# Retention and a gated feed-forward layer on one core: from full score matrices to 128-position chunks with a carried state

## The chip, the core and the metric

The kernel runs on one core of a Trainium2 chip. Five engines of that core work side by side, each through its own queue of instructions in order, and meet through semaphores: TensorE (PE) multiplies matrices, with the loads of its weights shown as a row of their own (PEld); VectorE (DVE), ScalarE (ACT) and GpSimd (POOL) work element by element; SyncE (SP) here only starts transfers. The transfers themselves run on 16 DMA engines. The metric is device time in microseconds for one execution.

## The reference

Inputs are q, k and v in fp32, shaped 8 batches x 8 heads x 576 positions x 64, and two weight matrices, 512 x 2048 and 2048 x 512. The output is 4608 x 512 in fp32.

```
scores = (q @ k.T) / 8                       # per batch and head
Dmat[i, j] = gamma_h ** (i - j)  if i >= j else 0,   gamma_h = 1 - 2 ** (-5 - h)
x = (scores * Dmat) @ v                      # then heads side by side: 4608 x 512
h = x @ w_in                                 # 4608 x 2048
g = h * clip(h + 3, 0, 6) / 6
out = g @ w_out                              # 4608 x 512
```

There is no softmax: a head's output is a causal sum in which older positions fade by a fixed factor per step.

## The kernel before

**Attention.** The kernel goes through batches, and in each batch through four pairs of heads (the loop over `c`). For a pair it loads q, k and v of both heads from DRAM with a cast to fp16 on the way (`cast_load`, line 97; the transfers are issued by POOL, one per head and tensor, 128 x 5 x 64 elements). TensorE transposes q and k in blocks of 128 positions (line 174), VectorE and ScalarE copy the transposes out of PSUM (lines 178, 180). Then the whole lower half of the 576 x 576 score matrix of each head is formed, transposed, in bands of 128 key positions (line 200); VectorE multiplies each band with a table of decay factors for every distance and head, `dmask`, and writes fp16 (line 210). The bands are multiplied with v (line 230), and ScalarE copies the result into `xt16`, which holds x transposed for all 4608 tokens (line 236). The two heads of a pair use rows 0 to 63 and 64 to 127 of the array in the score products, and columns 0 to 63 and 64 to 127 in the products with v.

**The table.** At the start POOL builds the distances (`rsel`) and ScalarE turns them into `dmask` with eight exponentials of 128 x 1600 elements (line 80).

**The feed-forward part.** Tokens are taken in nine blocks of 512. `moe_unit` with kind 0 is one up unit: four matmuls of 128 x 512 into one PSUM bank (line 122), a relu on ScalarE (line 126) and the gating on VectorE (line 128), which writes a slice of `gt16`. With kind 1 it is one down unit: 16 matmuls for 128 tokens (line 136), a copy by ScalarE (line 140) and a store of 256 KB (line 141, issued by SP). The weights are loaded by POOL in three pieces during the first batch, cast to fp16 on the way (lines 243, 246).

**Order.** `chunkq` is the list of units whose tokens are ready, and `pop_units` issues a few of them at fixed places between the parts of a head pair, so that TensorE has large matmuls beside attention. A block becomes ready only when the batch that holds its last token is finished. From this program order a scheduler derives the order on each engine. All PSUM tiles come from one pool of eight banks. What remains in `chunkq` after the last batch follows without attention beside it.

Of the kernel before, what the change touches and what calls it, by code (L numbers as in the profile page):

```python
# [14 lines left out]
ALU = mybir.AluOpType  # L15


@with_exitstack
def kernel(
# [13 lines left out]
    P = 128  # L33

    NCH = (S + P - 1) // P
    msz = [min(P, S - P * i) for i in range(NCH)]
    m1sub = []
    for tcix in range(NCH):
        lo = P * tcix
        subs = []  # L40
        while lo < S:
            hi = min(lo + 512, S)
            subs.append((lo, hi))
            lo = hi
        m1sub.append(subs)
    atoff = []
    o = 0
    for tcix in range(NCH):
        atoff.append(o)
        o += S - P * tcix  # L50
    ATW = o
    m2sc = [(0, 288), (288, 576)]

    gamma = [1.0 - 2.0 ** (-5.0 - h) for h in range(H)]
    NFULL = S // P
    REM = S - NFULL * P

    const = ctx.enter_context(tc.tile_pool(name="const", bufs=1))
    work = ctx.enter_context(tc.tile_pool(name="work", bufs=3))
    big = ctx.enter_context(tc.tile_pool(name="big", bufs=1))  # L60
# [3 lines left out]
    cb = const.tile([P, 2], FP32)  # L64
    nc.gpsimd.memset(cb[:, 0:1], 0.5)
    nc.gpsimd.memset(cb[:, 1:2], float(np.log(0.125)))

    rsel = const.tile([P, ATW], FP32)
    for tcix in range(NCH):
        W = S - P * tcix  # L70
        nc.gpsimd.iota(rsel[:, atoff[tcix]:atoff[tcix] + W],
                       pattern=[[1, W]], base=0, channel_multiplier=-1,
                       allow_small_or_imprecise_dtypes=True)
        nc.gpsimd.affine_select(
            out=rsel[:, atoff[tcix]:atoff[tcix] + W],
            in_=rsel[:, atoff[tcix]:atoff[tcix] + W], compare_op=ALU.is_ge,
            fill=1.0e8, base=0, pattern=[[1, W]], channel_multiplier=-1)
    dmask = const.tile([P, H, ATW], FP16)
    for h in range(H):
        nc.scalar.activation(dmask[:, h, :], rsel, ACTF.Exp,  # L80
                             bias=cb[:, 1:2], scale=float(np.log(gamma[h])))

    win16 = big.tile([P, DM // P, DFF], FP16)
    wout16 = big.tile([P, DFF // P, DM], FP16)

    NCC = DM // P
    xt16 = big.tile([P, NCC, NTOK], FP16)

    psum = ctx.enter_context(tc.tile_pool(name="psum", bufs=8, space=bass.MemoryType.PSUM))

    def cast_load(src4, b, h, dst, coloff, width):
        last = (b == B - 1 and h == H - 1)
        if not last:
            fl = src4[b, h].rearrange("s d -> (s d)")
            ap = bass.AP(tensor=fl.tensor, offset=fl.offset,
                         ap=[[D, P], [P * D, NCH], [1, D]])
            nc.gpsimd.dma_start(dst[:, :, coloff:coloff + D], ap)
        else:
            nc.gpsimd.dma_start(
                dst[:, 0:NFULL, coloff:coloff + D],  # L100
                src4[b, h, 0:NFULL * P, :].rearrange("(j p) d -> p j d", p=P))
            nc.gpsimd.dma_start(dst[0:REM, NFULL, coloff:coloff + D],
                                src4[b, h, NFULL * P:S, :])
            nc.gpsimd.memset(dst[REM:P, NFULL, coloff:coloff + D], 0.0)

    NFC = DFF // P
    MBLK = 512
    NMB = NTOK // MBLK
    chunkq = []
    moe_state = {}  # L110

    def moe_unit(kb, kind, ix):
# [30 lines left out]
    def pop_units(n):  # L143
        for _ in range(n):
            if chunkq:
                moe_unit(*chunkq.pop(0))
# [142 lines left out]
```

## Time and profile before

| | |
|---|---|
| three runs | 450.07, 449.37, 449.47 us; median 449.47 |
| the profiled execution | span 448.7 us from the first to the last instruction; its own time is not listed beside it |
| matmuls | 2368, of which 576 up and 576 down with 512 columns each |
| moved | read 39.80 MB, written 9.44 MB |
| loads of q, k, v and weights | issued by POOL, 129,488 packets |
| stores | issued by SP, 5184 packets, 36 transfers of 256 KB, 2.0 us to landing |

PE, PEld, DVE, ACT, POOL and SP are the engines' names in the profile; L122 is line 122 of the kernel. A row of the slices gives the busy tenths of an engine in 40 equal parts of the span; PEclk is the clock that TensorE was granted, in tenths of full speed. The chain is followed back from the last instruction, at each step to what released it. In a list of groups or a timeline, "out<-in" names the tiles, and "64*128 64x512" is a matmul on 64 rows and 128 columns of the array with 512 moving columns. A share of the DMA engines above 100% means that transfers overlap on them.

### The profile page before, as it was taken

What the parts mean: (1) busy time and instruction counts of PE and PEld (TensorE: products, weight loads), DVE (VectorE), ACT (ScalarE), POOL (GpSimd) and SP (SyncE); (2) the same over time, 40 slices, a digit from 0 to 9 for tenths busy, and PEclk for the clock granted to TensorE, in tenths of its full rate; (3) what the DMA queues carried; (4) which work ended last, traced back from release to release, by engine and by line L of the source; (5) the groups of instructions that cost most, each with busy time, mean ns of one, the idle gap of its engine ahead of it and who ended that gap; (6) DMA issues with size and microseconds to landing.
All of it is one profiled execution on the core that took longest, in us unless ns stands there. A gap on an engine that the chain in (4) does not pass through costs nothing.

```text
span 448.7 us, 6207 instructions
## 1 busy us (share of the span) xinstructions
PE 394.0 (88%) x2368; PEld 181.7 (40%) x2368; DVE 230.5 (51%) x432; ACT 201.6 (45%) x349; POOL 177.6 (40%) x222
## 2 busy tenths in 40 slices
PE   0387999989998999899998999899989999899996
PEld 0133444434443444444443444344443444344442
DVE  0254675347716672467635771667245763480540
ACT  5623564156522663356415652266325641571641
POOL 9966799763534444155326353445200000000000
PEclk9999999999998999999999999999998999999999
DMA  5999999985777766487568568776210001001101
GB/s 36 123 189 192 120 96 96 154 75 37 46 92 88 46 45 61 86 55 50 37 101 74 39 44 93 87 50 42 39 70 1 0 1 70 26 0 48 47 23 70
DMA packets 134700, 29.73 MB, mean 66 GB/s; under 512 B 126480, under 2 KB 130064, under 8 KB 134672
## 3 DMA queue, kind: packets, MB, share of 16 engines
q0 software_dynamic: 129488, 19.91, 60.8%
q1 hardware_dynamic: 5184, 9.44, 5.7%
q8 instruction: 18, 0.29, 0.3%
q14 instruction: 10, 0.08, 0.1%
HBM read 39.80 MB, written 9.44 MB: 110 GB/s over the span
## 4 chain that ended last, share of the span: by engine, by line
PE 69%; DVE 18%; ACT 9%; issue 2%; POOL 1%; DVEq 0%; POOLq 0%
PE pout L136 28%; PE ph L122 22%; DVE at16a L210 8%; DVE at16b L210 6%; PE pst L174 5%; ACT dmask L80 3%; ACT xt_104 L236 2%; ACT u L126 2%; ACT sb L180 2%; DVE gt_6_3580 L128 1%; DVE gt_5_3055 L128 1%; DVE gt_0_430 L128 1%; DVE gt_4_2530 L128 1%; DVE gt_3_2005 L128 1%; DVE gt_2_1480 L128 1%
## 5 line engine op out<-in xcount | busy, mean ns | idle before, releaser
L122 PE MATMUL ph<-xt_104,win_102 128*128 128x512 f16 x576 | 143.2, 383 | 5.7 <-DVE gt_1_955 L128 0.8
L126 ACT ACTIVATE u<-ph,cb 128x512 f32<-128x512 f32 x144 | 97.2, 687 | 53.2 <-PE ph L122 51.0
L122 PEld LDWEIGHTS <-win_102 128*128 128x128 f16 x576 | 52.6, 97 | 71.0 <-issue 19.5
L140 ACT COPY osb<-pout 128x512 f32<-128x512 f32 x36 | 21.1, 585 | 111.5 <-PE pout L136 111.5
L178 DVE COPY sb<-pst 128x576 f16<-128x576 f16 x32 | 14.5, 455 | 43.3 <-PE pst L174 43.3
L200 PEld LDWEIGHTS <-sb 64*128 64x128 f16 (+1 forms) x384 | 14.9, 100 | 42.5 <-ACT sb L180 18.2
L180 ACT COPY sb<-pst 128x576 f16<-128x576 f16 x32 | 20.4, 637 | 3.6 <-PE pst L174 1.6
L128 DVE SCALAR_TENSOR_TENSOR gt_8_4320<-u,ph 128x512 f16<-128x512 f32 x16 | 11.0, 688 | 16.6 <-ACT u L126 16.6
L128 DVE SCALAR_TENSOR_TENSOR gt_6_3580<-u,ph 128x512 f16<-128x512 f32 x16 | 10.7, 681 | 9.0 <-ACT u L126 8.9
L128 DVE SCALAR_TENSOR_TENSOR gt_2_1480<-u,ph 128x512 f16<-128x512 f32 x16 | 10.5, 679 | 9.2 <-ACT u L126 9.2
L128 DVE SCALAR_TENSOR_TENSOR gt_5_3055<-u,ph 128x512 f16<-128x512 f32 x16 | 10.7, 681 | 8.0 <-ACT u L126 7.8
L128 DVE SCALAR_TENSOR_TENSOR gt_4_2530<-u,ph 128x512 f16<-128x512 f32 x16 | 10.7, 681 | 8.0 <-ACT u L126 7.8
L128 DVE SCALAR_TENSOR_TENSOR gt_0_430<-u,ph 128x512 f16<-128x512 f32 x16 | 10.5, 680 | 8.3 <-ACT u L126 8.3
L128 DVE SCALAR_TENSOR_TENSOR gt_1_955<-u,ph 128x512 f16<-128x512 f32 x16 | 10.5, 680 | 8.1 <-ACT u L126 8.1
L128 DVE SCALAR_TENSOR_TENSOR gt_3_2005<-u,ph 128x512 f16<-128x512 f32 x16 | 10.5, 680 | 8.1 <-ACT u L126 8.1
L136 PE MATMUL pout<-wout_103,gt_2_1480 128*128 128x512 f16 x64 | 14.3, 379 | 0.2 <-DVE at16a L210 0.2
L136 PE MATMUL pout<-wout_103,gt_4_2530 128*128 128x512 f16 x64 | 14.3, 379 | 0.2 <-DVE at16a L210 0.2
L136 PE MATMUL pout<-wout_103,gt_0_430 128*128 128x512 f16 x64 | 14.3, 379 | 0.2 <-DVE at16a L210 0.2
L136 PE MATMUL pout<-wout_103,gt_1_955 128*128 128x512 f16 x64 | 14.3, 379 | 0.2 <-DVE at16a L210 0.2
L136 PE MATMUL pout<-wout_103,gt_5_3055 128*128 128x512 f16 x64 | 14.3, 379 | 0.2 <-DVE at16a L210 0.2
L136 PE MATMUL pout<-wout_103,gt_6_3580 128*128 128x512 f16 x64 | 14.3, 379 | 0.2 <-DVE at16a L210 0.2
L136 PE MATMUL pout<-wout_103,gt_3_2005 128*128 128x512 f16 x64 | 14.3, 379 | 0.2 <-DVE at16a L210 0.2
(1059 smaller groups left out, 775.9 us busy)
## 6 DMA issues: line engine op xcount, KB each, us to landing
out_dram<-osb SPq DMA_DIRECT2D x36, 256.0 KB, 2.0
win_102<-in_moe_w_in_dram POOLq DMA_DIRECT2D x2, 640.0 KB, 8.8
wout_103<-in_moe_w_out_dram POOLq DMA_DIRECT2D x2, 640.0 KB, 10.0
win_102<-in_moe_w_in_dram POOLq DMA_DIRECT2D x1, 768.0 KB, 9.9
wout_103<-in_moe_w_out_dram POOLq DMA_DIRECT2D x1, 768.0 KB, 10.5
qn_108<-in_q_dram POOLq DMA_DIRECT2D x2, 80.0 KB, 3.0
kn_109<-in_k_dram POOLq DMA_DIRECT2D x2, 80.0 KB, 3.0
vn_110<-in_v_dram POOLq DMA_DIRECT2D x2, 80.0 KB, 3.1
```

Source lines behind the costliest of these rows:

```text
L80: nc.scalar.activation(dmask[:, h, :], rsel, ACTF.Exp, bias=cb[:, 1:2], scale=float(np.log(gamma[h])))
L122: nc.tensor.matmul(ph, win16[:, dmc, P * fc:P * fc + P], xt16[:, dmc, tok0:tok0 + MBLK], start=(dmc == 0), stop=(dmc == NCC - 1))
L126: nc.scalar.activation(u, ph, ACTF.Relu, bias=cb[:, 0:1], scale=1.0 / 6.0)
L128: nc.vector.scalar_tensor_tensor(out=gt16[:, fc, :], in0=u, scalar=1.0, in1=ph, op0=ALU.min, op1=ALU.mult)
L136: nc.tensor.matmul(pout, gt16[:, fc, P * mc:P * mc + P], wout16[:, fc, :], start=(fc == 0), stop=(fc == NFC - 1))
L140: nc.scalar.copy(osb, pout)
L174: nc.tensor.transpose(pst[:, P * j:P * j + sj], nat[0:sj, j, :], ident16[0:sj, 0:sj])
L178: nc.vector.tensor_copy(sb, pst)
L180: nc.scalar.copy(sb, pst)
L200: nc.tensor.matmul(pms[h2][0:mt, co:co + ns], kt2[base:base + D, P * tcix:P * tcix + mt], qt2[base:base + D, a:bb], start=True, stop=True)
L210: nc.vector.tensor_tensor(out=at16s[h2][0:mtg, alo:alo + wid], in0=pms[h2][0:mtg, 0:wid], in1=dmask[0:mtg, 2 * c + h2, alo:alo + wid], op= ...
L236: nc.scalar.copy(xt16[h2 * D:h2 * D + D, c, b * S + s0:b * S + s1], pos[h2][h2 * D:h2 * D + D, 0:s1 - s0])
```

## The change

The attention part is written anew, and the order of the whole kernel with it.

The 4608 tokens are cut into 36 chunks of 128 positions. `load(c)` fetches k, q and v of a chunk for all eight heads in fp32, with SP issuing (256-byte rows; a chunk that lies across a batch border takes two transfers per tensor). `casts(c)` makes fp16: k on ScalarE, q on POOL (on VectorE for the first four chunks), v on POOL; q is multiplied with gamma^p/8 and v with gamma^-p, where p is the position in the chunk less 64, so that the decay inside the chunk comes out of the product itself and the mask holds only ones and zeros. `transposes(c)` makes q and k transposed: by TensorE for chunks 0 to 3, by a transposing DMA issued from SP for the others.

Inside a chunk, `scores(c)` and `inner(c)` do the causal product; what earlier chunks of the batch contribute comes from a 64 x 64 state per head. `state(c)` forms k^T v of the chunk, VectorE adds the previous state, POOL multiplies with gamma^128 (`gpow`) and copies the result into `sbd`, a block-diagonal fp16 tile for the two heads of a pair; `inner` of the next chunk multiplies it with q and adds it in PSUM. A chunk that lies across a batch border uses a second mask and, for its state, a second v whose first half is zero (`vz`).

`visit(c)` is the unit of order: it issues the loads up to chunk c+5, casts and transposes up to chunk c+1, the scores of c, the product with v of chunk c-1 and the state of c. The order on TensorE is that of the program throughout, on POOL only up to the first up product. Five visits come first, with the weight loads between them in 24 pieces; then the 16 up units of block 0 with a visit after every fourth; then, for each block, an up unit of the next block and four matmuls of the down product of this one in turn, with a visit after every fourth unit until chunk 36 is past. A down product holds two PSUM banks at a time and stores 512 KB per pair of 128-token tiles.

```diff
--- before
+++ after
...
+def segments(c):
+    n0 = P * c
+    b, s0 = divmod(n0, S)
+    if s0 + P <= S:
+        return [(b, s0, P, 0)]
+    m = S - s0
+    return [(b, s0, m, 0), (b + 1, 0, P - m, m)]
+straddle = [len(segments(c)) > 1 for c in range(NCH)]
+has_state = [segments(c)[0][1] > 0 for c in range(NCH)]
+gives_state = [c + 1 < NCH and has_state[c + 1] for c in range(NCH)]
+keeps_state = [has_state[c] and not straddle[c] for c in range(NCH)]
...
+io = ctx.enter_context(tc.tile_pool(name="io", bufs=4))
+work = ctx.enter_context(tc.tile_pool(name="work", bufs=3))
+gp = ctx.enter_context(tc.tile_pool(name="gp", bufs=6))
+psum = ctx.enter_context(tc.tile_pool(name="psum", bufs=8, space=bass.MemoryType.PSUM))
...
+arg = const.tile([P, 2 * H], FP32)
+dec = const.tile([P, 2 * H], FP32)
+nc.scalar.activation(dec, arg, ACTF.Exp)
...
+gpow = const.tile([P, NP], FP32)
...
+mask = const.tile([P, 2, P], FP16)
...
+sbd = []
...
+win16 = const.tile([P, NP, DFF], FP16)
+wout16 = const.tile([P, NFC, DM], FP16)
...
+def load(c):
+    tiles = []
+    for nm, src in (("k", k), ("q", q), ("v", v)):
+        t = io.tile([P, H, D], FP32, tag=f"f{nm}", name=f"f{nm}{c}")
+        for (b, s0, n, p0) in segments(c):
+            nc.sync.dma_start(t[p0:p0 + n], src[b, :, s0:s0 + n, :].rearrange("h s d -> s h d"))
+        tiles.append(t)
+    st[c] = dict(f=tiles)
+def casts(c):
+    fk, fq, fv = st[c]["f"]
+    k16 = work.tile([P, H, D], FP16, tag="k16", name=f"k16_{c}")
+    q16 = work.tile([P, H, D], FP16, tag="q16", name=f"q16_{c}")
+    v16 = work.tile([P, H, D], FP16, tag="v16", bufs=4, name=f"v16_{c}")
+    nc.scalar.copy(k16, fk)
+    qe = nc.vector if c < PE_T else nc.gpsimd
+    qe.tensor_tensor(q16, fq, dec[:, 0:H].unsqueeze(2).to_broadcast([P, H, D]), ALU.mult)
+    nc.gpsimd.tensor_tensor(v16, fv, dec[:, H:2 * H].unsqueeze(2).to_broadcast([P, H, D]), ALU.mult)
+    st[c].update(k16=k16, q16=q16, v16=v16, vz=v16)
+    if straddle[c] and gives_state[c]:
+        vz = work.tile([P, H, D], FP16, tag="vz", bufs=1, name=f"vz_{c}")
+        nc.gpsimd.tensor_tensor(vz, fv, decz.unsqueeze(2).to_broadcast([P, H, D]), ALU.mult)
+        st[c]["vz"] = vz
+def transposes(c, on_pe):
+    for nm in ("k", "q"):
+        src = st[c][nm + "16"].rearrange("p h d -> p (h d)")
+        dst = work.tile([P, NP, P], FP16, tag=f"{nm}T", name=f"{nm}T_{c}")
+        if on_pe:
+            pt = psum.tile([P, NP, P], FP16, tag="pp", name=f"pt{nm}{c}")
+            for i in range(NP):
+                nc.tensor.transpose(pt[:, i, :], src[:, i * P:(i + 1) * P], ident16)
+            nc.vector.tensor_copy(dst, pt)
+        else:
+            nc.sync.dma_start_transpose(dst, src)
+        st[c][nm + "T"] = dst
+def scores(c):
+    kT, qT = st[c]["kT"], st[c]["qT"]
+    a16 = work.tile([P, 2, NP, P], FP16, tag="a16", name=f"a16_{c}")
+    pa = [psum.tile([P, NP, P], FP32, tag="pp", name=f"pa{h2}_{c}") for h2 in range(2)]
+    for i in range(NP):
+        for h2 in range(2):
+            r = slice(h2 * D, h2 * D + D)
+            nc.tensor.matmul(pa[h2][:, i, :], kT[r, i, :], qT[r, i, :], start=True, stop=True)
+    m = mask[:, int(straddle[c]):int(straddle[c]) + 1, :].to_broadcast([P, NP, P])
+    for h2 in range(2):
+        nc.vector.tensor_tensor(a16[:, h2], pa[h2], m, ALU.mult)
+    st[c]["a16"] = a16
+def state(c):
+    if not gives_state[c]:
+        return
+    k16, vz = st[c]["k16"], st[c]["vz"]
+    pu = psum.tile([P, NP, 2, D], FP32, tag="pp", name=f"pu{c}")
+    for i in range(NP):
+        nc.tensor.matmul(pu[:, i], k16[:, 2 * i:2 * i + 2, :], vz[:, 2 * i:2 * i + 2, :],
+                         start=True, stop=True)
+    z = work.tile([P, NP, D], FP32, tag="z", bufs=2, name=f"z{c}")
+    g = gpow.unsqueeze(2).to_broadcast([P, NP, D])
+    t = work.tile([P, NP, D], FP32, tag="t", bufs=2, name=f"t{c}")
+    for h2 in range(2):
+        r = slice(h2 * D, h2 * D + D)
+        if keeps_state[c]:
+            nc.vector.tensor_tensor(t[r], pu[r, :, h2, :], prev_z[0][r], ALU.add)
+        else:
+            nc.vector.tensor_copy(t[r], pu[r, :, h2, :])
+    nc.gpsimd.tensor_tensor(z, t, g, ALU.mult)
+    prev_z[0] = z
+    s = sbd[(c + 1) % 2]
+    for h2 in range(2):
+        r = slice(h2 * D, h2 * D + D)
+        nc.gpsimd.tensor_copy(s[r, :, h2, :], z[r])
+def inner(c):
+    kb = c // 4
+    if kb not in xts:
+        xts[kb] = work.tile([P, NP, BLK], FP16, tag="xT", bufs=3, name=f"xT{kb}")
+    a16, v16, qT = st[c]["a16"], st[c]["v16"], st[c]["qT"]
+    po = psum.tile([P, NP, P], FP32, tag="pp", name=f"po{c}")
+    n = P // 2 if straddle[c] else P
+    s = sbd[c % 2]
+    for i in range(NP):
+        for h2 in range(2):
+            nc.tensor.matmul(po[h2 * D:h2 * D + D, i, :], v16[:, 2 * i + h2, :], a16[:, h2, i, :],
+               start=(i == 0), stop=not has_state[c], skip_group_check=True)
+    if has_state[c]:
+        for i in range(NP):
+            nc.tensor.matmul(po[:, i, 0:n], s[:, i], qT[:, i, 0:n],
+               start=False, stop=True, skip_group_check=True)
+    o = (c % 4) * P
+    nc.scalar.copy(xts[kb][:, :, o:o + P], po)
...
+def up_unit(kb, u):
+    jj, r = divmod(u, 4)
+    half_i, jr = divmod(r, 2)
+    fc = 2 * jj + jr + JH * half_i
+    if r == 0:
+        gt[kb, jj] = [gp.tile([P, 2, BLK], FP16, tag=f"g{x}", bufs=n, name=f"g{x}{kb}_{jj}")
+                      for x, n in (("a", 8), ("b", 8))]
+    g = gt[kb, jj][half_i]
+    ph = psum.tile([P, BLK], FP32, tag="pp", name=f"ph{kb}_{fc}")
+    for dmc in range(NP):
+        nc.tensor.matmul(ph, win16[:, dmc, P * fc:P * fc + P], xts[kb][:, dmc, :],
+                         start=(dmc == 0), stop=(dmc == NP - 1))
+    uu = work.tile([P, BLK], FP32, tag="u", bufs=3, name=f"u{kb}_{fc}")
+    nc.scalar.activation(uu, ph, ACTF.Relu, bias=half, scale=1.0 / 6.0)
+    nc.vector.scalar_tensor_tensor(out=g[:, jr, :], in0=uu, scalar=1.0, in1=ph,
+                     op0=ALU.min, op1=ALU.mult)
...
+def down_plain(kb):
+    for m2 in range(2):
+        pd = [psum.tile([P, DM], FP32, tag="pp", name=f"pd{kb}_{m2}{m}") for m in range(2)]
+        o = out_tile(kb, m2)
+        for jj in range(4):
+            for m in range(2):
+                t0 = P * (2 * m2 + m)
+                for hf in range(2):
+                    for jr in range(2):
+                        nc.tensor.matmul(pd[m], gt[kb, jj][hf][:, jr, t0:t0 + P],
+                           wout16[:, 2 * jj + jr + JH * hf, :],
+                           start=(jj == 0 and hf == 0 and jr == 0),
+                           stop=(jj == 3 and hf == 1 and jr == 1))
+                        yield
+        for m in range(2):
+            nc.scalar.copy(o[:, m, :], pd[m])
+        nc.sync.dma_start(out_pair(kb, m2), o)
+def win_piece(jj):
+    sl = lambda ap: ap.rearrange("p cc (h j f) -> p cc h j f", h=2, f=2 * P)[:, :, :, jj, :]
+    for dmc in range(NP):
+        nc.gpsimd.dma_start(sl(win16)[:, dmc], sl(win_v)[:, dmc])
+def wout_piece(jj):
+    for hf in range(2):
+        fc = JH * hf + 2 * jj
+        nc.gpsimd.dma_start(wout16[:, fc:fc + 2, :], wout_v[:, fc:fc + 2, :])
+PE_T = 4
+AHEAD = 6
...
+def visit(c):
+    fetch(c + AHEAD)
+    prepare(c + 2)
+    if c < NCH:
+        scores(c)
+    if 0 <= c - 1:
+        inner(c - 1)
+    if c < NCH:
+        state(c)
+with tc.manual_schedule(engines={ENG.PE}):
+    with tc.manual_schedule(engines={ENG.Pool}):
+        fetch(2)
+        prepare(1)
+        win_piece(0)
+        fetch(4)
+        prepare(2)
+        win_piece(1)
+        visit(0)
+        win_piece(2)
+        visit(1)
+        win_piece(3)
+        for c in range(2, 5):
+            wout_piece(c - 2)
+            visit(c)
+        wout_piece(3)
+    for u in range(NFC):
+        up_unit(0, u)
+        if u in (3, 7, 11, 15):
+            visit(5 + u // 4)
+    for kb in range(NB):
+        down = down_plain(kb)
+        base = 4 * (kb + 2) + 1
+        for u in range(NFC):
+            if kb + 1 < NB:
+                up_unit(kb + 1, u)
+            for _ in range(4):
+                next(down, None)
+            if u % 4 == 2 and kb + 2 < NB:
+                visit(base + u // 4)
+        for _ in down:
+            pass
```

## The prediction

> **What bounds the kernel now.** I read the busy times first, then the slices, then the chain that ended last, then the same chain in order of time, and last the DMA queues in a stretch where loads run flat out.
>
> The page: totals, the slices and the shares of the chain.
>
> ```profile
> span 448.7 us, 6207 instructions
> PE 394.0 (88%) x2368; PEld 181.7 (40%) x2368; DVE 230.5 (51%) x432; ACT 201.6 (45%) x349; POOL 177.6 (40%) x222
> PE   0387999989998999899998999899989999899996
> ...
> PEclk9999999999998999999999999999998999999999
> ...
> PE 69%; DVE 18%; ACT 9%; issue 2%; POOL 1%; DVEq 0%; POOLq 0%
> ```
>
> TensorE is busy in 88% of the span, at full granted clock, and carries 69% of the chain; the other 31% are moments in which it waits for VectorE or ScalarE inside attention. No other engine is above 51%.
>
> The chain in order of time gives the price of each kind of work (columns: start, length in us, what).
>
> ```profile
> 46.14 0.29 PE po_404 L230
> ...
> 47.88 0.54 PE ph L122 x2
> ...
> 247.75 0.82 PE pst L174 x10
> ...
> 252.18 0.60 DVE at16b L210
> 252.78 0.60 DVE at16a L210
> 253.38 0.60 DVE at16b L210
> ...
> 431.04 13.83 PE pout L136 x64
> ```
>
> 64 matmuls of 128x512 take 13.83 us: 216 ns each. Ten transposes of 128 columns, with a weight load each, take 0.82 us: 82 ns each. The first up matmul starts at 47.88, so everything before it is head; the masking runs of VectorE are waits of TensorE.
>
> TensorE's own timeline shows how two heads share the array (start, length, what).
>
> ```profile
> 250.34 0.39 PE L200 MATMUL pm_2614<-sb 64*128 64x512 f16 x1
> 250.34 0.39 PE L200 MATMUL pm_2615<-sb 64*128 64x512 f16 x1
> 250.56 0.19 PE L200 MATMUL pm_2620<-sb 64*128 64x64 f16 x1
> 250.56 0.19 PE L200 MATMUL pm_2621<-sb 64*128 64x64 f16 x1
> ```
>
> Matmuls of the two heads, on 64 rows each, start together and cost one. The DMA answer for 60 to 76 us, when only loads run:
>
> ```profile
> DMA packets 12260, 1.56 MB, mean 97 GB/s; under 512 B 12258, under 2 KB 12258, under 8 KB 12258
> q0 software_dynamic: 12258, 1.53, 150.9%
> ```
>
> 12,258 packets in 16 us are 766 per us, and POOL, which issued them back to back, set that pace: the rings can do at least this. Over the whole page the same queue shows 129,488 packets in 60.8% of 16 engines' 448.7 us: 33.7 ns of one engine per packet, overlaps counted twice, so at worst 475 per us.
>
> **The sum of before.** Up and down products: 1152 x 0.2158 = 248.6 us. Head to the first up matmul: 47.9. After the last matmul (444.9): copy 0.58, store, 3.8 in all. The rest, 448.7 - 248.6 - 47.9 - 3.8 = 148.4 us, is attention of the 28 head pairs after the first batch, waits included: 5.3 us per pair. The median of the runs is 449.47; the span is 0.8 below it, and I add 0.8 at the end.
>
> **The change, part by part.** The 1152 large matmuls stay: 248.6 us. Per 128-position chunk, `visit` now issues 24 matmuls of 128 columns: eight scores, eight products with v (both in pairs of half the array), four for the carried state, four for the new state. If a pair costs one, 16 x 82 ns = 1.3 us; if not, 24 x 82 = 2.0. Bare streaming would be 16 x 54 = 0.9. The pairs at 250.34 are nearest, so I take 1.3. Between a 512-column run and attention TensorE lost about 0.1 us (eight matmuls from 248.50 end at 250.23 by 216 ns each; scores start at 250.34); four such changes per visit make 1.7 us (ends 0.9 and 2.4). Five visits fall into the head and 31 after it: 31 x 1.7 = 52.7 us, in place of 148.4.
>
> The masking waits of before (the lines at16a and at16b) do not come back: the scores of chunk c are used by `inner` a whole visit later. Visits lie four up-and-down units apart, 4 x 8 x 0.216 = 6.9, plus 1.7: 8.6 us. In that time VectorE has 4 gatings (0.68), 2 masks (0.68) and 2 half-height state sums (bounded by 0.68): 5.4 at most. ScalarE has 4 relus (0.69) and 3 copies (0.59): 4.5. These are covered while visits stay 8.6 apart. In the first block of up products there is no down product beside them, and visits come 3.5 + 1.7 = 5.2 us apart; there VectorE's 5.4 is as long as TensorE's run. The state chain (two VectorE operations, the POOL scaling, two POOL copies, behind two POOL casts) is also about 5. I add 3 us there (0 to 8). Two down tiles hold a PSUM bank each for eight units; the other six serve four tiles of a visit and the up tiles, each free again after 0.69 + 0.68 us, so I add nothing.
>
> POOL: 192 of the old load issues at about 0.9 us leave. It gets per chunk the casts of q and v, the state scaling and two small copies. Its row nearest in shape, a select over 128x576 of fp32, took 0.66 us, and VectorE's 128x512 two-input multiply 0.60 to 0.68; POOL's simple pass is 1.45 times VectorE's (0.66 against the 0.455 of a 128x576 copy), which makes 1.0 us for a cast (ends 0.6 and, as two passes, 1.3), 1.1 for the state's three. About 3.1 us per visit of 8.6: covered.
>
> SP takes over 120 loads, 64 transposes and 18 stores of 512 KB. A chunk's three loads are 3 x 1040 packets of 256 B: 4.1 us at 766 per us, 6.6 at 475. No transpose by DMA is in the trace. As a copy of 512 packets it costs 0.7 us of the rings (1.1 at the worst rate); not overlapped with anything, it costs what an 80 KB load takes to land, 3.0 us. Nothing excludes more. I take the copy price, the nearest in packet size; the store's half share is 0.5 x 288 x 79 ns / 16 = 0.7 (5184 packets in 5.7%). So 4.1 + 1.4 + 0.7 = 6.2 us per chunk against 8.6: hidden. A store waits for ScalarE's second copy and holds the loads behind it; these are fetched four chunks (34 us) before their cast, so this costs nothing as long as the queue keeps up.
>
> Transposes are a place for the Trainium skill. Its page "DMA: Bandwidth & Descriptors", section "Latency and other measured facts", gives a DMA transpose 261 GB/s; for 128 KB that is an estimate of 0.5 us, and the sum would stand. No run here shows it so far.
>
> **The head.** ScalarE's decay factors stand behind the cast of the second chunk's k, the fourth load: 0.8 + 3.0 (landing) + 4 x 1.36 gives 9 us. From there POOL, whose order is written out, paces: four v casts (1.0 each), three state groups (1.1), 20 weight issues (512 to 683 descriptors took 0.79 to 0.87 us, so 0.7 for 256: 14), the q cast of chunk 4: 9 + 4 + 3.3 + 14 + 1 = 31. Its transpose (1 to 3) and visit 4 follow: 35. By then some 11 MB are read; before moved 185 to 200 GB/s of halved bytes from 20 to 45 us, twice that read, so 11 MB need 29 us of a full queue, and I add 5 for issues that wait for a slot. The up products begin at 40 (30 to 50), in place of 47.9.
>
> **Sum:** 40 + 248.6 + 52.7 + 3 + 3.8 = 348.1 span, 349 us.
>
> **The rivals.** A is this sum, TensorE-bound. With single ends exchanged it runs from 325 (head 30, visit 1.3) to 378 (head 50, visit 2.2, stalls 6).
>
> B: the queue paces. At 33.7 ns a packet, loads 6.6, transposes 2.2, store 0.7 make p = 9.5 us per chunk. Visits 5 to 36 then take 32 p; after the last one 1.7 + 27.6 + 13.8 + 3.8 = 47 remain: 40 + 304 + 47 + 0.8 = 392. For it: one queue carries everything, in order, and a transpose waits on casts of two engines. Against it: the 766 of the fence was POOL's pace and not the rings'.
>
> C, slower: each transpose empties the queue, so that its 3.0 us lie bare: 6.6 + 6.0 + 0.7 = 13.3 per chunk, 40 + 426 + 47 + 0.8 = 514. It decides from p = 11.3, where 40 + 32 p + 47 reaches 449: with loads at 4.1 that is 3.2 us per transpose. For it: two transposes per chunk on the queue that also feeds them. Against it: today's loads overlap freely (150.9% busy). The Trainium skill speaks for it in "VectorE: DVE Perf Modes", section "The three transpose paths": 1309 ns for a 128x128 by DMA against 390 by TensorE. Four blocks would make an estimate of 5.2 us a transpose, p = 15.3 and 577 us. No row here bears it out yet.
>
> D: pairs and weight loads overlap fully and the head is short: 30 + 248.6 + 31 x 0.9 + 3.8 + 0.8 = 311; anything below 325.
>
> **How the numbers follow.** A 0.70, B 0.15, C 0.11, D 0.04; the time is A's. The range 325 to 405 holds A and two thirds of B, 0.80. Faster by over 0.2% (about what a measurement of this kernel can tell from no change): A, D and B, less 0.01 for B near 449: 0.88; within: 0.01; slower: C, 0.11.
>
> **What would show it.** Right: the first up matmul near 40; 34.5 us per block of four visits with 216 ns per large matmul; 1.7 us from the first score to the next up matmul; VectorE nowhere on the chain but in the first block; transposes landing in under 3 us. Wrong: score matmuls that wait for a DMA, SP waiting for its own earlier transfers, visits more than 9 us apart (B), or 11.3 and more (C); casts of POOL well over 1.3 us would move the head and the first block.

## The result and the profile after

The changed kernel takes 355.75 us (median of four, 354.29 to 357.04) beside 449.77 for the kernel before on the same chip: a ratio of 0.7865, with a 95% interval of 0.7799 to 0.7931. The forecast of 349 was 1.9% low, inside its range of 325 to 405. The profiled execution took 357.04 us with a span of 355.3; the sum made 348.1 of span, so 7.2 us have to be explained, and it will turn out that they are the rest of two larger errors of opposite sign.

The page of the changed kernel: totals, the slices of TensorE and of its granted clock, and the shares of the chain that ended last.

```profile
span 355.3 us, 5554 instructions
PE 303.1 (85%) x2016; PEld 148.1 (42%) x2016; DVE 175.7 (49%) x322; ACT 161.1 (45%) x254; POOL 137.9 (39%) x202
PE   0550008699999999999999999999999999999994
PEclk9995557879999999999999999999999999999999
PE 81%; DMA 10%; DVE 3%; SPq 2%; ACT 2%; POOL 1%; issue 1%; ACTq 0%
```

From the ninth slice to the last but one TensorE is busy 90% of the time or more, and VectorE with ScalarE have gone from 27% of the chain to 5%: the masking waits of before are gone. But in slices four to six (27 to 53 us) TensorE stands still, and a new 10% of the chain belongs to transfers. The chain in order of time says which (start, length in us, what).

```profile
49.87 1.76 SPq L140
51.74 2.48 DMA qT<-q
56.74 4.49 PE ph L217 x16
62.54 6.67 DMA qT<-q
71.49 5.57 PE ph L217 x16
...
83.50 1.02 PE ph L217 x4
...
335.94 14.69 PE pd L241 x68
```

The up products begin at 56.74, not at 40. The second block begins at 83.50, after another transfer into a transposed q, with 6.67 us on the chain, for which TensorE stood 3.54 us. From there to 350.63, where the last run of down products ends, no wait of a microsecond is on the chain. SyncE's timeline shows how the first transpose came to be issued at 49.87 (start, length of the issue, what).

```profile
28.89 5.04 SPq L111 DMA_DIRECT2D fk<-in_k_dram  x1
34.03 4.22 SPq L111 DMA_DIRECT2D fq<-in_q_dram  x1
...
49.87 1.76 SPq L140 DMA_TRANSPOSE kT<-k  x1
```

SP works its list in order. The two transposes of chunk 4 stand behind all loads of chunks 0 to 8, 27 tensors. While the DMA engines write 203 to 214 GB/s without a break (20 to 45 us), the issue of one load stretches from about 0.5 us to 5.04, and SP's waits for semaphores, at most 8.3 us in all from 20 to 52 us, are the smaller part of its delay. The q cast of chunk 4 on POOL was finished at 32.6, close to the 31 of the prediction; its transpose was issued 17 to 19 us later, with nothing missing but its turn. TensorE's row for the scores of chunk 4 carries the price in brackets (idle time before it, and what ended it).

```profile
54.35 0.61 PE L150 MATMUL pa<-qT,kT 64*128 64x128 f16 x8 [25.07 <-DMA qT<-q]
```

Once everything runs, a visit is shorter than forecast. TensorE's timeline of one visit: scores, product with v, carried state, new state, next up products.

```profile
161.42 0.40 PE L150 MATMUL pa<-qT,kT 64*128 64x128 f16 x8
161.75 0.41 PE L194 MATMUL po<-a,v 128*64 128x128 f16 x8
162.09 0.40 PE L198 MATMUL po<-qT,sbd 128*128 128x128 f16 x4
162.33 0.39 PE L164 MATMUL pu<-v,k 128*128 128x128 f16 x4
162.55 1.03 PE L217 MATMUL ph<-xT,win 128*128 128x512 f16 x4
```

From the first score to the next up matmul pass 1.13 us (start to start; the lengths shown overlap because the ends are modelled). Over the 28 visits behind 83.50 (the last is only a product with v) the mean is (350.63 - 83.50 - 1088 x 0.2158) / 28 = 1.15 us, in place of 1.7.

### The profile page after: what moved, and what is told of

The parts are those of the page before. It is cut to its first block, busy times and chain, and to the rows that moved or that the text cites. A ratio compares the mean times of both kernels' runs of the same rounds, so it can differ in the third digit from the quotient of the medians.

```text
span 355.3 us, 5554 instructions
## 1 busy us (share of the span) xinstructions
PE 303.1 (85%) x2016; PEld 148.1 (42%) x2016; DVE 175.7 (49%) x322; ACT 161.1 (45%) x254; POOL 137.9 (39%) x202
## 4 chain that ended last, share of the span: by engine, by line
PE 81%; DMA 10%; DVE 3%; SPq 2%; ACT 2%; POOL 1%; issue 1%; ACTq 0%
PE pd L241 35%; PE ph L217 34%; DMA fk<-in_k_dram 4%; PE po L194 3%; PE pa L150 3%; DMA fq<-in_q_dram 3%; PE po L198 3%; DMA qT<-q 3%; PE pu L164 2%; SPq L111 1%; DVE q L122 1%; DVE a L153 1%; PE ptq L137 1%; ACT k L120 1%; SPq L140 1%
## 5 line engine op out<-in xcount | busy, mean ns | idle before, releaser
L217 PE MATMUL ph<-xT,win 128*128 128x512 f16 x576 | 148.9, 385 | 1.0 <-ACT xT L201 1.0
L220 ACT ACTIVATE u<-ph,half 128x512 f32<-128x512 f32 x144 | 98.9, 687 | 97.9 <-PE ph L217 97.4
L241 PE MATMUL pd<-wout,ga 128*128 128x512 f16 x288 | 85.7, 379 | 0.0
L241 PE MATMUL pd<-wout,gb 128*128 128x512 f16 x288 | 85.7, 379 | 0.0
L221 DVE SCALAR_TENSOR_TENSOR ga<-u,ph 128x512 f16<-128x512 f32 x72 | 49.4, 688 | 70.3 <-ACT u L220 70.2
L217 PEld LDWEIGHTS <-win 128*128 128x128 f16 x576 | 55.9, 99 | 63.7 <-issue 5.2
L221 DVE SCALAR_TENSOR_TENSOR gb<-u,ph 128x512 f16<-128x512 f32 x72 | 49.5, 688 | 49.7 <-ACT u L220 49.3
L123 POOL TENSOR_TENSOR v<-fv,dec 128x512 f16<-128x512 f32 x36 | 37.5, 1042 | 85.6 <-PE po L194 59.1
L153 DVE TENSOR_TENSOR a<-pa,mask 128x512 f16<-128x512 f32 x72 | 46.4, 683 | 28.3 <-PE pa L150 27.9
L122 POOL TENSOR_TENSOR q<-fq,dec 128x512 f16<-128x512 f32 x32 | 33.3, 1041 | 29.9 <-DMA qT<-q 19.7
L120 ACT CAST k<-fk 128x512 f16<-128x512 f32 x36 | 22.2, 620 | 26.8 <-DMA fk<-in_k_dram 25.7
L175 POOL TENSOR_TENSOR z<-t,gpow 128x256 f32<-128x256 f32 x32 | 19.6, 611 | 33.8 <-DVE t L172 28.1
```

Of the source, the lines that this page charges most:

```text
L120: nc.scalar.copy(k16, fk)
L122: qe.tensor_tensor(q16, fq, dec[:, 0:H].unsqueeze(2).to_broadcast([P, H, D]), ALU.mult)
L123: nc.gpsimd.tensor_tensor(v16, fv, dec[:, H:2 * H].unsqueeze(2).to_broadcast([P, H, D]), ALU.mult)
L153: nc.vector.tensor_tensor(a16[:, h2], pa[h2], m, ALU.mult)
L217: nc.tensor.matmul(ph, win16[:, dmc, P * fc:P * fc + P], xts[kb][:, dmc, :], start=(dmc == 0), stop=(dmc == NP - 1))
L220: nc.scalar.activation(uu, ph, ACTF.Relu, bias=half, scale=1.0 / 6.0)
```

## The experiments

Three things were to be told apart. First, the late head: is it the order of SP's queue (the theory formed from the trace above), or the bytes that have to be moved anyhow? Second, the price of a transposing DMA, on which rivals B and C stand. Third, whether the pairs of half-array matmuls and the interleaving of up and down products are worth what the prediction assumed. Times of single runs are compared with the 355.75 of the change; the intervals of the ratios reach 1 to 3 us to each side, so differences of that size are read from the starts in the traces, which are those of the profiled executions.

**Transposes of chunks 4 to 7 on TensorE.** This takes them out of SP's queue in the head.

```diff
+    PE_X = 8
-            transposes(c, c < PE_T)
+            transposes(c, c < PE_X)
```

> Only the transposes of chunks 4 to 7 move from the transposing DMA to TensorE (the q casts stay where they are). Theory Q (the transposes of chunk 4 stand in SP's queue behind the loads of chunks up to 8, some 7.1 MB beside 4.2 MB of weights at 212 GB/s, and that sets the first up product at 56.7): POOL's q cast of chunk 4 ends at 32.6, so the up products begin at 37 to 40; the transposes of chunk 8 become the next wait, near 64; in all 335 to 343 us. Theory B (the loads themselves are late, bytes bound the head whatever the order): up products still begin at 50 or later, 350 to 357 us.

Measured: 349.85 us (348.64 to 350.99), ratio 0.7758 [0.7701, 0.7816]. TensorE's timeline of this run, its first up products, and the scores of chunk 8 behind them:

```profile
44.87 4.13 PE L217 MATMUL ph<-xT,win 128*128 128x512 f16 x16 [0.25 <-ACT xT L201]
...
72.48 0.61 PE L150 MATMUL pa<-qT,kT 64*128 64x128 f16 x8 [8.01 <-ACT k L120]
```

The head shrinks by 11.9 us, and 8.0 us come back at chunk 8, the first whose transposes are in SP's queue again: its kT was issued at 67.83 and its qT at 69.72, behind loads as before. (The bracket names a cast of ScalarE that belongs to a later chunk and had itself waited for this kT; the two transfers landed at 71.78 and 72.34.) The wait moved with the first transposing DMA. Theory B, with up products at 50 or later, is out, but Theory Q was too hopeful: the up products begin at 44.87 and not at 37 to 40, and the time lies above its 335 to 343. Ahead of them TensorE stands 4.97 us for the q cast of chunk 5, whose transposes now come before the scores of chunk 4 in TensorE's order.

**All transposes on TensorE.** The same line with 36 in place of 8.

> All 36 chunks are transposed by TensorE, no transposing DMA is left. Theory Q: the head is that of e1, 37 to 40; each visit after it gets eight transposes more, 8 x 0.08 = 0.65 us, 20 us in all, and VectorE two copies of 0.42; 344 to 352 us. Theory B: head 50 or later and the same 20 us: 365 to 375 us. If the transposing DMAs cost time in the steady part as well, it is below 340.

Measured: 352.48 us (351.95 to 353.70), ratio 0.7826 [0.7760, 0.7892]. This is 0.5 us above Theory Q's 344 to 352, with a head longer than its 37 to 40. TensorE's timeline, from the transposes of chunk 5 to the first up products:

```profile
41.55 0.61 PE L137 MATMUL ptq<-ident,q 128*128 128x128 f16 x4 [3.10 <-POOL q L122]
42.09 0.61 PE L150 MATMUL pa<-qT,kT 64*128 64x128 f16 x8
...
44.48 4.66 PE L217 MATMUL ph<-xT,win 128*128 128x512 f16 x16 [0.25 <-ACT xT L201]
```

The up products begin at 44.48, the second block at 66.65, with no wait of a microsecond in the first block. So 12.2 of the head's 16.7 us of excess go when no transpose is in SP's queue. The other 4.5 are not a share of the change's own delay: they are the price of this order, in which TensorE transposes chunk 5 ahead of the scores of chunk 4 and so waits for the q of chunk 5, whose load landed at 40.3. Behind 66.65 the rest of the span is 350.1 - 66.65 = 283.4 us, 11.6 more than the 271.8 of the change behind 83.50: eight more TensorE instructions for each of 26 chunks, 0.45 us per chunk. That is what the transposing DMAs save once the head is past.

**Loads four chunks ahead in place of six.** The transposes of chunk 4 then stand behind the loads up to chunk 6.

```diff
-    AHEAD = 6
+    AHEAD = 4
```

> AHEAD is 4 and not 6, so the transposes of chunk 4 stand behind the loads of chunks up to 6 and not 8: 1.6 MB less in front of them. Theory Q: up products begin 7 us earlier, near 49; 346 to 351 us. Theory B: no change of the head, 354 to 360 us, longer if the loads now come too late in the steady part.

Measured: 350.29 us (348.44 to 351.39), ratio 0.7764 [0.7705, 0.7823]. kT of chunk 4 is issued at 41.77, 8.1 us earlier, the up products begin at 50.82, 5.9 earlier, and the time falls by 5.5, inside what Theory Q expected. Only positions in SP's queue were changed, no byte and no instruction. With this the order of the queue as the cause is shown twice, by taking the transposes out and by taking loads from in front of them.

**The second weight matrix behind visits 5 to 8.**

```diff
             for c in range(2, 5):
-                wout_piece(c - 2)
                 visit(c)
-            wout_piece(3)
...
                 visit(5 + u // 4)
+                wout_piece(u // 4)
```

> The loads of the second weight matrix move behind visits 5 to 8. Theory Q: 1.6 MB written (3.1 MB read) less in front of the transposes of chunk 4: up products 7 to 10 us earlier; 343 to 350 us if the first block does not pay it back. A third theory P (POOL's written-out list sets the head): four to six issues of 0.75 us less, so 3 to 4 us earlier, 352.

Measured: 356.57 us (356.01 to 357.58), ratio 0.7910 [0.7855, 0.7965]; no verdict on the theory, since the edit did not do what it was meant to. Outside the part in which POOL's order is written out, the scheduler placed these transfers as early as it could, the first at 1.73 us. The weights came ahead of the loads, and the up products began at 61.98.

**Transposes of chunks 4 to 11 on TensorE.** The first edit with 12 in place of 8.

> The edit: chunks up to 11 are transposed by TensorE, transposing DMAs begin with chunk 12. Theory (the order of SP's queue in the head makes the first transposing DMAs late; once loads have caught up, they are hidden): the up products begin near 45 as with 8 chunks, the first block then runs without the wait of 8.0 us for chunk 8, so that the second begins near 67 instead of 74.9; four more chunks with eight TensorE transposes each cost 4 x 0.66 = 2.6 us, and the transposes of chunk 12 are not needed before some 90 us. Sum: 349.9 - 8.0 + 2.6 = 344 us (341 to 348). Rival (loads, not transposes, are late in the first block): the block ends near 73 all the same and the time stays within 1 us of 350.

Measured: 341.99 us (341.33 to 342.31), ratio 0.7590 [0.7569, 0.7611]. The up products begin at 45.38 and the second block at 67.58; kT of chunk 12 is issued at 88.8 and nobody waits for it. The theory held: the time is 2 us below its sum and inside its range.

**Each transposing DMA from chunk 12 on issued twice.** This adds work; the copies are read by nobody.

```diff
                 nc.sync.dma_start_transpose(dst, src)
+                if c >= 12:
+                    tw = work.tile([P, NP, P], FP16, tag=f"{nm}W", name=f"{nm}W_{c}")
+                    nc.sync.dma_start_transpose(tw, src)
```

> The edit: from chunk 12 on each transposing DMA is issued twice, the second time into a tile that nobody reads; this is work added. Visits lie 8.06 us apart in steady state. Theory of the prediction (a transpose costs the rings what a copy of 512 packets does, 0.7 us): a chunk asks 4.1 + 4 x 0.7 + 0.7 = 7.6 us of the rings, still hidden, and the time stays at 356 us (354 to 359). Rival 1 (SP's issue time is the next limit): four issues of 1.2 to 1.6 us, three loads of 0.5 to 1.1 us and a quarter of two stores make 7 to 10 us per chunk; from 8.06 on it paces, at 9 it adds 25 x 0.9 = 23 us, 379. Rival 2 (each transpose empties the queue, 3.0 us bare): 4.8 + 12 = 16.8 us per chunk, 356 + 25 x 8.7 = 574.

Measured: 379.39 us (378.33 to 381.48), ratio 0.8431 [0.8396, 0.8467]: as rival 1 had it. SyncE's timeline of one chunk, first transpose to first transpose:

```profile
183.12 2.52 SPq L140 DMA_TRANSPOSE kT<-k  x1
185.69 1.26 SPq L143 DMA_TRANSPOSE kW<-k  x1
187.05 1.21 SPq L140 DMA_TRANSPOSE qT<-q  x1
188.31 1.26 SPq L143 DMA_TRANSPOSE qW<-q  x1
...
191.91 2.40 SPq L140 DMA_TRANSPOSE kT<-k  x1
```

8.8 us from chunk to chunk, of which the issues shown and three loads (0.53, 0.58, 0.89) fill 8.25; over 20 chunks from 101.72 on the mean is 9.0. SP has no pause left: from 90 to 290 us its pauses of over 0.2 us add up to 3.0 us, where the change has 54.4, while visits want a chunk every 8.08 us. The DMA engines are not what is full (mean busy share 0.92 from 100 to 140 us and 0.93 from 180 to 218, where the change has 1.09 and 0.82; in the head of the change it reaches 1.36), and kT lands after 4.0 us in the median in both. TensorE does not pay this chunk by chunk. For a while visits stay as far apart as in the change, on buffers; then ScalarE's cast of a later k waits for the added transpose that still reads the buffer (10.3 us in the first case), the relus stand behind the cast, and TensorE stands still:

```profile
152.85 0.59 PE L167 MATMUL pu<-v,k 128*128 128x128 f16 x4 [6.00 <-DVE ga L224]
...
234.86 1.87 PE L220 MATMUL ph<-xT,win 128*128 128x512 f16 x4 [11.45 <-ACT xT L204]
```

With one more wait of 1.50 us and matmuls at half speed behind the two long ones this is the loss. The added transposes cost 23.6 us for 48, and what runs out is issue time on SP, not time of the rings.

**The half-array matmuls not next to each other.** In `scores` and `inner` all matmuls of the first heads come before all of the second.

```diff
-        for i in range(NP):
-            for h2 in range(2):
+        for h2 in range(2):
+            for i in range(NP):
```

> The edit: in scores and in the product with v, the matmuls of all first heads come before those of all second heads, so that neighbours use the same half of the array. Theory (a pair of half-array matmuls costs one, 83 ns): eight pairs of a visit become 16 single matmuls of 55 to 83 ns, 0.88 to 1.33 us in place of 0.66; 0.2 to 0.7 us in each of 28 visits after the first block, so 362 to 376 us. Rival (the pairs gain nothing, visits are short because weight loads overlap): within 1 us of 356.

Measured: 356.49 us (355.76 to 357.94), ratio 0.7921 [0.7896, 0.7946]: 0.7 us from the change, well within the intervals and far from the theory's 362 to 376, and eight scores pass in 0.34 us as against 0.33. Either the pairs gain nothing, or the two halves run side by side even when their matmuls are four places apart. The single starts speak for the second: of the eight scores from 161.95 on, two have started by 161.99, four by 162.04 and six by 162.10. The last experiment tests it.

**Up and down products not interleaved.** The whole down product follows the 16 up units with their four visits.

```diff
                 if kb + 1 < NB:
                     up_unit(kb + 1, u)
-                for _ in range(4):
-                    next(down, None)
```

> The edit: the four down matmuls after each up unit are left to the end of the block, so that each block is 16 up units with four visits, then 64 down matmuls in one run; the work is the same. Theory (the down products beside the visits cover VectorE and the chain of the state): visits then lie 4 x 0.86 + 1.15 = 4.6 us apart, while VectorE has 4 gatings (2.7), two masks (1.37) and two state sums (0.83), 4.9 us; TensorE waits 0.3 us or more per visit, with the chain behind each visit 0.3 to 1.0, so 28 x 0.3 to 1.0 = 8 to 28 us more, 364 to 384 us. Rival (the buffers of PSUM and of the gated tiles even it out within a block): 355 to 358 us.

Measured: 360.96 us (360.53 to 361.64), ratio 0.8018 [0.7998, 0.8037], between the two expectations. The chain in order of time:

```profile
100.58 2.54 DMA qT<-q
105.41 13.81 PE pd L241 x64
...
123.04 3.45 PE ph L217 x16
127.62 3.45 PE ph L217 x16
```

Up units with visits follow each other at 4.6 us without a wait, and VectorE is busy 14.6 of the 18.6 us of such a stretch. Behind 105.41 are left 16 x 64 matmuls, 24 visits and the tail: 221.0 + 24 x 1.15 + 4.7 = 253.3 us; the span leaves 253.2. So interleaving hides nothing of VectorE; what the run loses (5.2 us by the medians, 3.3 by the spans of the profiled executions) it loses ahead of 105.41, where the second block asks for four chunks in some 18 us while SP's queue is still behind, and TensorE waits for qT again.

**The second weight matrix late, in POOL's written order.** With twelve chunks transposed by TensorE, and with the first up block taken into the part whose POOL order is written out.

```diff
+    PE_X = 12
...
             for c in range(2, 5):
-                wout_piece(c - 2)
                 visit(c)
-            wout_piece(3)
-        for u in range(NFC):
-            up_unit(0, u)
-            if u in (3, 7, 11, 15):
-                visit(5 + u // 4)
+            for u in range(NFC):
+                up_unit(0, u)
+                if u in (3, 7, 11, 15):
+                    visit(5 + u // 4)
+                    wout_piece(u // 4)
```

> The edit: chunks up to 11 transposed by TensorE, and the eight transfers of the second weight matrix are issued by POOL behind visits 5 to 8, in its written-out order, in place of ahead of visits 2 to 5. Theory (with the transposes out of SP's queue the head is set by the bytes that the rings have to write before chunk 5 is there, at some 212 GB/s): 4.7 MB of chunks 0 to 5 and 2.1 MB of the first weight matrix need 32 us in place of 42 with both matrices, so the up products begin near 36 (34 to 39) in place of 45, and the time falls by the same 7 to 10 us, to 332 to 335 us. Rival (loads of later chunks or POOL's list take the place of the weights): the up products begin at 42 or later and the time is 339 to 342.

Measured: 345.00 us (343.86 to 345.85), ratio 0.7636 [0.7591, 0.7681]. The up products begin at 39.68, 5.7 us earlier, and the second block at 67.82, no earlier than the 67.58 of the run with twelve chunks. Neither expectation holds: the head shrank nearly as the theory had it (39.68 against 34 to 39), but the time, 345.00, lies above its 332 to 335 and above the rival's 339 to 342. TensorE's timeline and POOL's, in the first block of this run:

```profile
58.76 0.40 PE L137 MATMUL ptq<-ident,q 128*128 128x128 f16 x4 [1.69 <-POOL q L122]
```

```profile
54.66 0.61 POOL L175 TENSOR_TENSOR z<-t,gpow 128x256 f32<-128x256 f32 x1 [1.95 <-DVE t L172]
55.34 0.83 POOL L180 CAST sbd<-z 64x256 f16<-64x256 f32 x2
56.11 1.48 POOL L259 DMA_DIRECT2D wout<-in_moe_w_out_dram  x2
57.67 1.03 POOL L122 TENSOR_TENSOR q<-fq,dec 128x512 f16<-128x512 f32 x1
```

A loop has closed: the q cast of the next chunk stands behind the state scaling and two weight issues in POOL's order, the state scaling waits for TensorE, and TensorE waits for the cast. Visits come 7.0 us apart (51.76, 58.76, 65.75).

**The same with loads four ahead.** `AHEAD = 4` on top.

> The edit: the one before, and loads four chunks ahead in place of six. Theory: once no transposing DMA stands behind loads in the head, the distance of the loads matters little there; within 2 us of the run without it. Rival 1 (loads of chunks 6 to 8 share the rings with chunk 5 and hold it up): the up products begin 2 to 4 us earlier and the time is 2 to 4 us lower. Rival 2 (four ahead is too near when the second weight matrix comes in between): TensorE waits for casts in the first or second block, 3 to 8 us more.

Measured: 345.57 us (344.53 to 347.40), ratio 0.7655 [0.7604, 0.7706], as the theory had it: with no transposing DMA behind the loads, their distance does not matter.

**Casts one visit earlier.** On top of the run with the second weights late, loads six ahead: from visit 3 on the casts of a chunk are ordered one visit ahead of its transposes, so that the q cast stands before the state scaling that would hold it (the first number of `prepare` now counts casts, the second transposes).

```diff
-        prepare(c + 2)
+        prepare(c + (3 if c >= 3 else 2), c + 2)
```

> The edit: that of the second weight matrix behind visits 5 to 8, and from visit 3 on the casts of a chunk stand one visit ahead of its transposes, so that in POOL's written-out order the q cast of the next chunk no longer stands behind the state scaling of the chunk before. Theory (late weights gave back in the first block what they saved in the head, since each visit then waited for POOL's z, then the q cast, then the transposes, 7.0 us from visit to visit): visits of the first block come 5.3 to 5.8 us apart, the up products begin near 37 to 39, the second block near 60 to 62 in place of 67.6, and the time is 334 to 337 us. Rival (the rings are still the bound through the first block, with both weight matrices and the loads of chunks 6 to 11 to be written by its end): the second block begins at 65 or later and the time is 340 to 343.

Measured: 335.25 us (334.45 to 336.22), ratio 0.7368 [0.7340, 0.7396]. The chain in order of time:

```profile
37.91 4.86 PE ph L217 x16
...
60.17 1.02 PE ph L217 x4
```

Up products from 37.91, visits 5.0 to 5.1 us apart, second block at 60.17, and nothing given back. This version beats both kernels; what it gains on the change, 20 us, it gains ahead of the second block, since the rest of the span is 333.0 - 60.17 = 272.8 us against 271.8.

**Scores of the first heads alone.** This leaves out the second heads' score matmuls; both masks read the first heads' scores, so that VectorE's work stays, and x is built from wrong scores for half of the heads.

```diff
-            for h2 in range(2):
+            for h2 in range(1):
...
-            nc.vector.tensor_tensor(a16[:, h2], pa[h2], m, ALU.mult)
+            nc.vector.tensor_tensor(a16[:, h2], pa[0], m, ALU.mult)
```

> The edit: four of the eight score matmuls of a visit are left out, those of the second head of each pair (rows 64 to 127); the masks of both heads then read the first heads' scores, so x comes from wrong scores for half of the heads and the work of VectorE stays. Theory (two matmuls on different halves of the array cost one, whether they stand next to each other in the order or not): four score matmuls take as long as the eight did, 0.33 us from their first start to the next group's, visits stay 8.06 us apart and the time stays at 355 to 357 us. Rival (each half-array matmul has its own price of 41 ns): four take 0.17 us less, 0.17 in each of 28 visits behind the first block, 350 to 351 us, and visits 7.9 us apart.

Measured: 357.14 us (355.71 to 357.71), ratio 0.7878 [0.7823, 0.7933]. TensorE's timeline of one visit, scores and product with v:

```profile
161.13 0.40 PE L150 MATMUL pa<-qT,kT 64*128 64x128 f16 x4
161.45 0.41 PE L194 MATMUL po<-a,v 128*64 128x128 f16 x8
```

Four score matmuls take 0.32 us, as long as eight did (0.33). A pair costs one; and with the run in which the heads were apart, it need not stand side by side in the order.

## Why the prediction was right, and where its steps were wrong

**The bound and the sign.** Right: TensorE carries the chain, the masking waits are gone, large matmuls stay at 0.2158 us, VectorE appears on the chain in the head and the first block alone. A's mechanism is what happened. Shares of the chain, taken times the spans, give an estimate of what the change is worth by engine: VectorE and ScalarE lose some 103 us of the chain (27% of 448.7, 5% of 355.3), TensorE some 22 (69% and 81%), and transfers with SP take up some 43 (12%). No run here separates the first two by an experiment. (The ends of A add up to 326.5 and 377.4, where the prediction has 325 and 378.)

**The head: predicted 40, measured 56.74, 16.7 too little.** What failed is an omission: the step priced what chunk 4 needs and not what SP has to issue ahead of its transposes. `fetch` runs six chunks ahead, so loads of chunks 5 to 8 stand before them. "I add 5 for issues that wait for a slot" was the only allowance. POOL's list, which the step took as the pace, ended when it was said to (cast of chunk 4 at 32.6 against 31; 1.04 us for a cast against 1.0; 0.72 per weight issue against 0.7), and the first weight matrix was in by 33.8 (issued by 25.4 and landed within 8.4 us). Had the transposes been issued at 32.6 and the rest taken the 6.9 us that it took (49.87 to 56.74), the up products would have begun at 39.5. By this estimate the whole 16.7 us are the wait for SP's turn. The step had a second fault: "By then some 11 MB are read" was divided by twice the rate of before, whose written bytes were halved by the cast. The fp32 loads of the change are not halved; from 20 to 45 us the DMA engines write 203 to 214 GB/s in all. Chunks 0 to 4 and both matrices are 3.9 + 4.2 = 8.1 MB written, 40 us at 205 GB/s, where the prediction had 29. This did not hold up chunk 4, whose loads stand early in the queue, but it makes each place in the queue long, and it is what the runs with transposes on TensorE run into with chunk 5.

**The visits: 1.7 us each, measured 1.15; over 27 visits behind the first block 13.6 us too much.** "If a pair costs one" was right, as the run with half of the scores shows. The size was wrong: 82 ns was the price of a transpose of before with its weight load, but within the groups of a visit pairs and full matmuls follow at about 56 ns (eight in 0.33 us, four in 0.24), close to the bare streaming that the prediction named as its lower end. And the array is switched three times at about 0.1 us, not four: between carried and new state nothing is lost (162.33 to 162.55 is 0.22 for four).

**The first block: 13.8 + 4 x 1.7 + 3 predicted, 26.8 measured, 3.2 too little.** The stalls are of another kind than thought, not VectorE's 5.4 us per visit but SP's queue still catching up: 3.54 us in which TensorE stands for qT, and a slow start of TensorE behind the wait. VectorE was overpriced, as the run without interleaving shows.

**The tail: 4.7 in place of 3.8.** The last store is 512 KB, which takes 3.4 us to land in the median, and was priced by the 2.0 of a 256 KB store.

Together: +16.7 + 3.2 - 13.6 + 0.9 = 7.2 us, the difference of the spans. That the median came within 1.9% owes something to the opposite signs.

**Rivals B and C.** Visits in steady state lie 8.08 us apart (mean from 88.78 to 298.80), set by TensorE, and it is SP that waits: 54.3 us in 25 waits ahead of transposes that the trace puts down to TensorE's up products. B (9.5) and C (13.3) were wrong for this kernel: a transpose takes 2.4 to 8.1 us to land, but the landings overlap. Doubling the transposes did make the queue pace at 9.0, by issue time on SP, which the prediction had not priced. With loads and store at the prediction's own prices, that run leaves (9.0 - 4.1 - 0.7) / 4 = 1.05 us at most of the rings for a transpose, beside the 0.7 taken. The estimate of 5.2 us from the Trainium skill ("VectorE: DVE Perf Modes", section "The three transpose paths") is not borne out as a cost per transpose: four in a chunk of 9.0 us leave less than half of that for each. The estimate of 0.5 us from the 261 GB/s of the Trainium skill ("DMA: Bandwidth & Descriptors", section "Latency and other measured facts") lies within the bound.

**What would have shown it.** The list named "score matmuls that wait for a DMA" as a sign against the forecast; this sign appeared, but in the head and the first block alone, where it is a delay of the start and not the pace. "Transposes landing in under 3 us" stood as a sign for it, and kT took 4.0 us in the median (qT 2.7): the sign was badly chosen, since landings overlap.

## What to carry to other kernels

Before pricing a step on an in-order queue, count what the program issues ahead of it on that queue, prefetches included: a load that is fetched early for chunk c+5 is a delay for the transpose of chunk c. Where early and late needs share one queue, put the first few urgent steps on another engine until the prefetch has caught up, then let the queue have them; and when an order is written out, look for the loop in which an engine's next cast stands behind work that waits for that cast. Price small matmuls from matmuls of their own kind in a run, and count the switches between kinds apart.

## What the runs showed of the hardware

- An issue on SP of a load with 256-byte rows takes 0.5 to 0.6 us in steady state and up to 6.5 us in the stretch in which the DMA engines write over 200 GB/s without a break (5.04 in the change, 6.03 in the run with loads four ahead, 6.47 in the run with four more chunks on TensorE). That the rings are full then is the likely reason and was not tested by itself. An engine that only issues can thus be the one that is late.
- A transposing DMA of 128x512 fp16 holds SP for 1.2 to 1.6 us in the median (qT, kT), twice a plain load's issue or more.
- The two halves of the array work through their matmuls side by side over at least four places of program order. The Trainium skill ("TensorE: Matmul & The Clock Gate", section "The mechanism") describes such overlap for tiles of the array; the runs add that halves need not alternate.
- Behind a wait TensorE can run at half speed for a few microseconds: in the run with the second weights late, four up matmuls took 1.74 us at 67.82 (1.74 / 4 = 0.43 us each) and 0.86 a few microseconds later. The first 16 up matmuls behind such a wait cost 4.1 to 5.6 us in place of 3.45 in the runs shown. Not every wait does it: behind the 0.77 us ahead of 83.50 the change runs at full speed at once. The Trainium skill ("TensorE: Matmul & The Clock Gate", section "What's actually happening") has half the rate until the array was busy for some 3.4 us. The trace agrees in the size of the step: its records of the granted clock have the half clock from 68.0 to 71.4 in that run and, twice as long, from 68.8 to 75.6 in the change, and the slow matmuls end where the record does. Where a trace has no record yet, the page shows 1.00: where all transposes are on TensorE the first record is the change to full at 46.6, the page reads 1.00 throughout, and the first 16 up matmuls take 4.66 us all the same.
